# Four late heads of a clustered attention with queries on partitions, an exact maximum and weights transposed by DMA

## The chip, the cores and the metric

One core of one Trainium2 chip. The metric is the device time in microseconds. Engines are named as in the profile: PE (matmuls), DVE (vector), ACT (activations), POOL (GpSimd), SP (which issues most DMAs).

## The reference

```python
def _attn_ref(q, k, v, centroids):          # B, H, S, D = 4, 8, 768, 64; 16 centroids a head
    ...
    q_assign = np.argmax(np.einsum('bhsd,hcd->bhsc', q_n, c_n), axis=-1)
    k_assign = np.argmax(np.einsum('bhsd,hcd->bhsc', k_n, c_n), axis=-1)
    mask = q_assign[:, :, :, None] == k_assign[:, :, None, :]
    scores = scale * np.matmul(q, k.transpose(0, 1, 3, 2))
    scores = np.where(mask, scores, -1000000000.0)
    scores = scores - np.max(scores, axis=-1, keepdims=True)
    attn = np.exp(scores)
    attn = attn / (np.sum(attn, axis=-1, keepdims=True) + 1e-09)
    return np.matmul(attn, v)
def _moe_ref(x, w_in, w_spatial, b_spatial, w_out):   # x: B, 768, 512; d_ff 1024
    h = np.maximum(x @ w_in, 0.0)
    u, v = (h[..., :d_ff // 2], h[..., d_ff // 2:])
    ...                                                # v_n: v normalised over its 512 columns
    v_s = np.einsum('ts,bsd->btd', w_spatial, v_n) + b_spatial[None, :, None]
    return ((u * v_s) @ w_out)
```

The output of the attention, heads side by side, is x of the second function.

## The kernel before, in words

The work is cut into 16 pairs of heads (n = 0 to 15, four pairs a batch, head number 2n + h) and, for each batch, one gated MLP. Every f32 operand is split into two f16 halves (high and low), and a product is made of three f16 products.

For a pair, `prep` loads keys and queries (`raw`), splits them (`hq`, `lo`), computes the logits against the centroids into a PSUM bank (`misc`), takes from them one-hot rows on DVE, and writes these rows into `hq` beside the 64 columns of the head. So one matmul gives the score with a penalty where the clusters differ. For pair 0 the two heads go through this one after the other, for the others together.

`shifts` makes, for every query, a maximum that keeps the exponential in range: nine times a head PE fills a PSUM bank with f16 scores (line 817, twelve matmuls) and DVE reduces it (line 824). The result goes through ACT into small columns, is transposed by a DMA on SP, and is copied into `hq` as one more row, so that the score matmuls subtract it.

`attend` runs a head in six blocks (k) of 128 keys. PE writes scores with keys on partitions and 768 queries in columns (lines 879 and 881) into one of two two-bank PSUM tiles (`sc`), ACT takes the exponential into an f32 tile (`p32`, line 885), ACT casts it to the high half (`pt`, line 887), POOL subtracts for the low half (line 888), and PE multiplies both with the values (line 893, eighteen matmuls a block, with six more for a mean correction at k = 0), for six groups of queries in one bank. Then DVE normalises, ACT and POOL split the result (`xhl`), and SP transposes it by DMA into `xT`.

`mlp` takes `xT` of a batch: tiles of v and u (`win`), the spatial product (`wsp`), u times it on DVE, a split and a DMA transpose (`gT`; in the last batch in `pt`'s buffers), the last product (`wou`), a scaling on ACT (line 1012) and a store from ACT's queue (line 1013). MLP matmuls are issued in groups of six and stand between the attention of later batches.

What decides the order: each engine executes its instructions in the order in which they stand, and that order is the table `ORDER`, a list of operation numbers per engine, written out in the file. Buffers rotate; a DMA on SP whose data isn't ready holds everything behind it on SP.

The names that matter below: `ROW` does not exist before; `r_p32` has three tiles (`P32_BUFS`), `r_o32`, the output tile, has one; `r_gT` has three; `misc` is one bank for both heads of pair 0.

Of the kernel before, what the change touches and what calls it, by code (L numbers as in the profile page):

```python
# [1084 lines left out]
```

## Time and profile before

| | |
|---|---|
| median of 3 runs | 664.67 us (662.88 to 666.4) |
| profiled execution | 662.72 us |
| its span, first to last instruction | 660.9 us |
| mean granted clock of PE | 0.989 |
| busy: PE, DVE, ACT, POOL | 626.0, 423.0, 445.9, 425.8 us |

A busy time is the sum over the whole span; the stages of the kernel have different limits, so the table is read together with the stretches below. The 1.8 us between span and time lie around the instructions.

### The profile page before, as it was taken

What the parts mean: (1) busy time and instruction counts of PE and PEld (TensorE: products, weight loads), DVE (VectorE), ACT (ScalarE), POOL (GpSimd) and SP (SyncE); (2) the same over time, 40 slices, a digit from 0 to 9 for tenths busy, and PEclk for the clock granted to TensorE, in tenths of its full rate; (3) what the DMA queues carried; (4) which work ended last, traced back from release to release, by engine and by line L of the source; (5) the groups of instructions that cost most, each with busy time, mean ns of one, the idle gap of its engine ahead of it and who ended that gap; (6) DMA issues with size and microseconds to landing.
All of it is one profiled execution on the core that took longest, in us unless ns stands there. A gap on an engine that the chain in (4) does not pass through costs nothing.

```text
span 660.9 us, 16698 instructions
## 1 busy us (share of the span) xinstructions
PE 626.0 (95%) x6769; PEld 376.4 (57%) x6769; DVE 423.0 (64%) x835; ACT 445.9 (67%) x759; POOL 425.8 (64%) x305
## 2 busy tenths in 40 slices
PE   1897889999999999999999999999999999999997
PEld 0475557666566655567654666656645655544443
DVE  6989999999699978279775775855545511132010
ACT  3695899996789848599955997758447675323212
POOL 2265789997589937587944987758635776424111
PEclk9987999999999999999999999999999999999999
DMA  4555866578556578575754155623210322301214
GB/s 147 146 133 136 195 140 159 128 166 192 128 130 128 122 157 178 117 165 109 149 138 67 27 102 114 134 57 82 43 25 18 69 62 25 88 17 48 64 33 127
DMA packets 104349, 70.49 MB, mean 107 GB/s; under 512 B 89432, under 2 KB 90640, under 8 KB 104272
## 3 DMA queue, kind: packets, MB, share of 16 engines
q1 hardware_dynamic: 100528, 62.73, 44.1%
q10 hardware_dynamic: 3744, 6.69, 3.0%
q8 instruction: 53, 0.87, 0.5%
q14 instruction: 24, 0.20, 0.1%
HBM read 27.63 MB, written 6.29 MB: 51 GB/s over the span
## 4 chain that ended last, share of the span: by engine, by line
PE 76%; DVE 18%; ACT 2%; issue 1%; DMA 1%; POOL 0%; SPq 0%; DVEq 0%; ACTq 0%
PE acc L938 41%; PE acc L893 12%; DVE nm L824 8%; PE acc L817 7%; PE sc L879 7%; PE sc L881 7%; DVE lo L675 1%; DMA out_dram<-o 1%; ACT p L885 1%; DVE vhl L761 1%; DVE xn L914 1%; DVE acc L607 1%; PE acc L704 1%; PE acc L706 1%; DVE acc L725 1%
## 5 line engine op out<-in xcount | busy, mean ns | idle before, releaser
L888 POOL TENSOR_TENSOR pt<-p,pt 128x768 f16<-128x768 f32 x192 | 322.5, 1704 | 49.6 <-ACT pt L887 35.1
L824 DVE TENSOR_REDUCE nm<-acc 128x1 f32<-128x512 f32 (+1 forms) x288 | 183.1, 681 | 28.8 <-PE acc L817 27.4
L885 ACT ACTIVATE p<-sc 128x768 f32<-128x768 f32 x192 | 153.0, 806 | 21.8 <-PE sc L881 16.8
L887 ACT CAST pt<-p 128x768 f16<-128x768 f32 x192 | 156.3, 830 | 2.1
L893 PEld LDWEIGHTS <-pt 128*128 128x128 f16 x3456 | 128.0, 98 | 28.8 <-issue 4.5
L893 PE MATMUL acc<-vhl,pt 128*128 128x65 f16 (+1 forms) x3456 | 136.7, 194 | 0.5 <-POOL pt L888 0.4
L938 PE MATMUL acc<-win,xT 128*128 128x512 f16 x576 | 129.4, 379 | 0.0
L817 PE MATMUL acc<-hq 80*128 80x256 f16 (+1 forms) x384 | 101.2, 340 | 11.0 <-DVE nm L824 7.6
L938 PE MATMUL acc<-vn,wsp 128*128 128x512 f16 x432 | 100.1, 379 | 0.0
L879 PE MATMUL sc<-hq,lo 128*128 128x512 f16 (+1 forms) x384 | 94.8, 328 | 1.1 <-ACT p L885 1.0
L881 PE MATMUL sc<-hq 81*128 81x512 f16 (+1 forms) x384 | 95.0, 328 | 0.7 <-DVE hq L855 0.7
L938 PEld LDWEIGHTS <-xT 128*128 128x128 f16 x576 | 55.7, 98 | 65.4 <-issue 0.5
L1004 POOL TENSOR_TENSOR ghl<-u,ghl 128x512 f16<-128x512 f32 x24 | 28.9, 1203 | 69.4 <-ACT ghl L1003 53.1
L1002 DVE SCALAR_TENSOR_TENSOR u<-acc,bsp,u 128x512 f32<-128x512 f32 x24 | 18.0, 749 | 86.1 <-PE acc L938 86.0
L938 PEld LDWEIGHTS <-wsp 128*128 128x128 f16 x432 | 41.0, 97 | 46.0
L881 PEld LDWEIGHTS <-hq 81*128 81x128 f16 x384 | 37.7, 98 | 26.8 <-issue 1.7
L817 PEld LDWEIGHTS <-hq 80*128 80x128 f16 x384 | 34.2, 100 | 29.5 <-issue 13.2
L675 DVE SCALAR_TENSOR_TENSOR lo<-raw,hq 128x768 f16<-128x768 f32 x30 | 37.2, 1250 | 21.3 <-ACT hq L666 21.3
L938 PE MATMUL acc<-wou,gT 128*128 128x512 f16 x216 | 50.4, 379 | 0.0
L917 POOL TENSOR_TENSOR xhl<-xn,xhl 128x384 f16<-128x384 f32 x32 | 30.5, 954 | 26.9 <-ACT xhl L916 26.8
L879 PEld LDWEIGHTS <-lo 128*128 128x128 f16 x384 | 33.8, 98 | 23.2 <-issue 6.0
L979 POOL TENSOR_TENSOR vn<-v,vn 128x512 f16<-128x512 f32 x24 | 28.5, 1201 | 24.1 <-ACT vn L978 24.1
(112 smaller groups left out, 598.7 us busy)
## 6 DMA issues: line engine op xcount, KB each, us to landing
raw<-in_kqT_dram SPq DMA_DIRECT2D x15, 768.0 KB
vraw<-in_vp_dram SPq DMA_DIRECT2D x16, 384.0 KB
out_dram<-o ACTq DMA_DIRECT2D x24, 256.0 KB
hq<-hq SPq DMA_DIRECT2D x15, 384.0 KB
hq<-lo SPq DMA_DIRECT2D x16, 192.0 KB
lo<-hq SPq DMA_DIRECT2D x16, 192.0 KB
wraw<-in_wsT_dram SPq DMA_DIRECT2D x6, 384.0 KB
vn<-in_w_in_dram SPq DMA_DIRECT2D x4, 512.0 KB
```

Of the source, the lines that this page charges most:

```text
L675: los.append(op("DVE", 0.95, lambda h=h: V.scalar_tensor_tensor(out=lo.t[:, h, :], in0=raw.t[:, h, :], scalar=QK_SCALE, in1=hq.t[:, 0, h, ...
L817: T.matmul(out=acc.t[:, c:c + cs.stop - cs.start], lhsT=hq.t[0:R_SH, 1, h, t * P:(t + 1) * P], rhs=hq.t[0:R_SH, 0, h, cs], start=c == 0, s ...
L824: V.tensor_reduce(out=nm.t[:, t, k:k + 1] if n == 1 else nm.t[:, t:t + n, k], in_=src, axis=AX.X, op=ALU.max, negate=True)
L879: T.matmul(out=sc.t[:, cs], lhsT=lo.t[:, h, ks], rhs=hq.t[:, 2, h, cs], start=True, stop=False)
L881: T.matmul(out=sc.t[:, cs], lhsT=hq.t[0:R_E, 0, h, ks], rhs=hq.t[0:R_E, 1, h, cs], start=False, stop=True)
L885: o = op("ACT", 0.81, lambda sc=sc, p32=p32: A.activation(out=p32.t, in_=sc.t[:, 0:S], func=AF.Exp, bias=P_LOG * LN2, scale=SC_UNIT), afte ...
L887: o = op("ACT", 0.83, lambda pt=pt, p32=p32: A.copy(out=pt.t[:, 0, :], in_=p32.t), after=[o], use=[p32], new=[pt], key=K_HI)
L888: o = op("POOL", 1.65, lambda pt=pt, p32=p32: G_.tensor_tensor(out=pt.t[:, 1, :], in0=p32.t, in1=pt.t[:, 0, :], op=ALU.subtract), after=[o ...
L893: T.matmul(out=av.t[:, t * (D + 1):t * (D + 1) + w], lhsT=lhsT, rhs=rhs, skip_group_check=True, **f)
L917: xls.append(op("POOL", 0.92, lambda xn=xn, hs=hs: G_.tensor_tensor(out=xhl.t[:, :, 1, hs], in0=xn.t, in1=xhl.t[:, :, 0, hs], op=ALU.subtr ...
L938: T.matmul(out=acc.t, lhsT=lr[m][0], rhs=lr[m][1], start=(m == 0), stop=(m == n - 1))
L1004: l = op("POOL", 1.16, lambda: G_.tensor_tensor(out=ghl.t[:, 1, :], in0=u32.t, in1=ghl.t[:, 0, :], op=ALU.subtract), after=[h], use=[u32, ...
```

## The change

Four heads (25, 27, 29 and 31, the second heads of the pairs of the last batch) go another way through `attend`, and `shifts` leaves them out. PE writes their scores with 128 queries on partitions and 768 keys in columns; DVE takes the exact maximum of a block; two one-element DVE operations make from it the scale and the bias of the exponential (a scale of zero where a query has no key in its cluster); ACT and POOL make the two halves as before; SP transposes both by one DMA, 128 by 1536, back into the buffer of the f32 tile; PE takes the transposed halves as its stationary operand, eighteen matmuls a block. The mean correction is not made for these heads. There is a fourth `p32` tile. The logits of pair 0's second head go into a bank of their own. A half copy of `hq` in pair 0 now reads ACT's copy. The output tile is gone: the scaled output is written over the `gT` tile that PE has read. The order of all engines is new.

```diff
-P32_BUFS = 3
+P32_BUFS = 4
...
-O_BUFS = 1
+ROW = (25, 27, 29, 31)
...
 ORDER = {
...
+    r_rs = R(sm, "rs", [P, 4], F32, 4)
...
-    r_o32 = R(moe, "o32", [P, DM], F32, O_BUFS)
...
-            qa2 = [sp(lambda: nc.sync.dma_start(out=hq.t[0:D, 2], in_=hq.t[D:P, 0]), 0.9, after=his, use=[hq], key=KQ)]
+            qa2 = [sp(lambda: nc.sync.dma_start(out=hq.t[0:D, 2], in_=hq.t[0:D, 1]), 0.9, after=qa0, use=[hq], key=KQ)]
...
+            if one and not first:
+                misc = r_acc.new()
...
         for h in range(2):
+            if 2 * n + h in ROW:
+                continue
             nm, sx = r_nm.new(), r_shx.new()
...
-            for k in range(NT):
+            for k in range(NT if 2 * n + h in ROW else 0):
+                plan.due = due(n, (6 * h + k) / 12)
+                sc, p32, pt, rs = r_sc.new(), r_p32.new(), r_pt.new(), r_rs.new()
+
+                def scores(sc=sc, h=h, k=k):
+                    ks = slice(k * P, (k + 1) * P)
+                    for cs in halves:
+                        T.matmul(out=sc.t[:, cs], lhsT=hq.t[:, 2, h, ks], rhs=lo.t[:, h, cs], start=True, stop=False)
+                    for cs in halves:
+                        T.matmul(out=sc.t[:, cs], lhsT=hq.t[0:R_SH, 1, h, ks], rhs=hq.t[0:R_SH, 0, h, cs], start=False, stop=True)
+
...
+                o = op("DVE", 0.95, lambda sc=sc, rs=rs: V.tensor_reduce(out=rs.t[:, 0:1], in_=sc.t[:, 0:S], axis=AX.X, op=ALU.max, negate=True), after=[o], use=[sc], new=[rs], key=K_MAX)
+                o = op("DVE", 0.16, lambda rs=rs: V.tensor_scalar(out=rs.t[:, 1:2], in0=rs.t[:, 0:1], scalar1=LIM, scalar2=SC_UNIT, op0=ALU.is_lt, op1=ALU.mult), after=[o], use=[rs], key=K_MAX)
+                o = op("DVE", 0.16, lambda rs=rs: V.tensor_scalar(out=rs.t[:, 2:3], in0=rs.t[:, 0:1], scalar1=rs.t[:, 1:2], scalar2=P_LOG * LN2, op0=ALU.mult, op1=ALU.add), after=[o], use=[rs], key=K_MAX)
+                o = op("ACT", 0.81, lambda sc=sc, p32=p32, rs=rs: A.activation(out=p32.t, in_=sc.t[:, 0:S], func=AF.Exp, bias=rs.t[:, 2:3], scale=rs.t[:, 1:2]), after=[o], use=[sc, rs], new=[p32], key=K_EXP)
...
+                o = op("POOL", 1.65, lambda pt=pt, p32=p32: G_.tensor_tensor(out=pt.t[:, 1, :], in0=p32.t, in1=pt.t[:, 0, :], op=ALU.subtract), after=[o], use=[p32, pt], key=K_LO)
+
+                def rt(p32=p32):
+                    return p32.t.bitcast(F16).rearrange("p (j q) -> p j q", q=P)
+
+                o = sp(lambda pt=pt, rt=rt: nc.sync.dma_start_transpose(rt(), pt.t.rearrange("p a s -> p (a s)")), 1.95, after=[o], use=[pt, p32], turn=True, key=K_XD)
+
+                def values(av=av, rt=rt, h=h, k=k):
...
+                    for j in range(NT):
+                        mm(j, D + 1, vh.t[:, j, h, 0:D + 1], start=k + j == 0, stop=False)
+                        mm(j, D, vh.t[:, j, h, D + 2:], start=False, stop=False)
+                        mm(NT + j, D + 1, vh.t[:, j, h, 0:D + 1], start=False, stop=j == NT - 1)
...
+            for k in range(0 if 2 * n + h in ROW else NT):
...
-            o32 = r_o32.new()
+
+            def o32():
+                return gT.t.rearrange("p a s -> p (a s)")[:, 0:2 * DM].bitcast(F32)
+
...
-            o = op("ACT", 0.6, lambda: A.activation(out=o32.t, in_=acc.t, func=AF.Copy, scale=2.0 ** -(G_LOG + WOUT_LOG)), after=[o], use=[acc], new=[o32], key=T_O)
-            op("ACT", 0.06, lambda: A.dma_start(out=out[b, t * P:(t + 1) * P, :], in_=o32.t), after=[o], use=[o32], dma=0.8, key=0)
+            o = op("ACT", 0.6, lambda: A.activation(out=o32(), in_=acc.t, func=AF.Copy, scale=2.0 ** -(G_LOG + WOUT_LOG)), after=[o], use=[acc, gT], key=T_O)
+            op("ACT", 0.06, lambda: A.dma_start(out=out[b, t * P:(t + 1) * P, :], in_=o32()), after=[o], use=[gT], dma=0.8, key=0)
```

The rest of the diff is the new table and some cost numbers of the planner that prints it; the table alone decides the order. Three places show how the order moves. Lines of the changed kernel are some 2 to 40 higher than those of the same code before (675 stays, 723 to 727 become 725 to 729, 824 becomes 828, 858 and 859 become 862 and 863, 919 becomes 958, 1005 becomes 1044).

The first is DVE at the start of the program, from the chain on the centroids' norms (p_114 holds the centroids) to the first one-hot steps on the logits. Before:

```order
L559 TENSOR_SCALAR p_114<-p_114,ninv 128x128
L675 SCALAR_TENSOR_TENSOR lo<-raw,hq 128x768
L568 CAST cmh<-acc_110 64x2x16
...
L569 TENSOR_TENSOR cml<-acc_110,cmh 64x6x16
L675 SCALAR_TENSOR_TENSOR lo<-raw,hq 128x768
L723 TENSOR_REDUCE mx<-acc_111 128x12
L724 TENSOR_TENSOR acc_111<-acc_111,mx 128x12x16
L725 TENSOR_TENSOR acc_111<-acc_111,wt 128x12x16
L723 TENSOR_REDUCE mx<-acc_111 128x12
```

And of the change:

```order
L559 TENSOR_SCALAR p_114<-p_114,ninv 128x128
L675 SCALAR_TENSOR_TENSOR lo<-raw,hq 128x768 x2
L568 CAST cmh<-acc_110 64x2x16
...
L569 TENSOR_TENSOR cml<-acc_110,cmh 64x6x16
L725 TENSOR_REDUCE mx<-acc_111 128x12
L726 TENSOR_TENSOR acc_111<-acc_111,mx 128x12x16
L727 TENSOR_TENSOR acc_111<-acc_111,wt 128x12x16
L725 TENSOR_REDUCE mx<-acc_112 128x12
```

The second low half stands directly behind the first, ahead of the placing of the centroids (cmh, cml), and the second head's logits are read from a second bank (acc_112).

The second place is DVE in the last batch, at the second head of pair 14 (head 29). Before, these are the last of its reductions and the step that joins them:

```order
L824 TENSOR_REDUCE nm_90<-acc_112 128x2
L824 TENSOR_REDUCE nm_90<-acc_111 128x1
L785 TENSOR_SCALAR wh_92<-acc_113 2x2x64
L824 TENSOR_REDUCE nm_90<-acc_110 128x1
L786 SCALAR_TENSOR_TENSOR w_8741<-acc_113,wh_92 2x2x64
L824 TENSOR_REDUCE nm_90<-acc_110 128x2
L836 TENSOR_REDUCE nl<-nm_90 128x6
```

In the change, behind the step that joins the first head's of pair 15:

```order
L840 TENSOR_REDUCE nl<-nm_90 128x6
L887 TENSOR_REDUCE rs<-sc_108 128x1
L888 TENSOR_SCALAR rs<-rs 128x1
L889 TENSOR_SCALAR rs<-rs 128x1
L887 TENSOR_REDUCE rs<-sc_109 128x1
L787 TENSOR_SCALAR wh_92<-acc_110 2x2x64
L951 TENSOR_SCALAR rc<-acc_111 128x6
L888 TENSOR_SCALAR rs<-rs 128x1
L952 RECIPROCAL rc<-rc 128x6
L889 TENSOR_SCALAR rs<-rs 128x1
```

The reductions from the four banks (acc) are gone; DVE now stands between the scores (sc) and the exponential, with three instructions a block.

The third place is SP at the end of the last batch, pair 15. Before:

```order
L788 DMA mean_86<-wh_92 1x2x65
L858 DMA_TRANSPOSE sht<-shx_84 128x6x128
L1005 DMA_TRANSPOSE gT<-ghl 128x8x128
L859 DMA hq<-sht 3x768
L789 DMA mean_86<-wl_94 1x2x65
L919 DMA_TRANSPOSE xT_104<-xhl 128x12x128
L1005 DMA_TRANSPOSE gT<-ghl 128x8x128 x3
L919 DMA_TRANSPOSE xT_104<-xhl 128x12x128
```

And of the change (p_9059 and the like are the f32 tiles that take the transposed halves):

```order
L1044 DMA_TRANSPOSE gT<-ghl 128x8x128
L958 DMA_TRANSPOSE xT_104<-xhl 128x12x128
L898 DMA_TRANSPOSE p_9059<-pt 128x12x128
L898 DMA_TRANSPOSE p_9092<-pt 128x12x128
L898 DMA_TRANSPOSE p_9143<-pt 128x12x128
L1044 DMA_TRANSPOSE gT<-ghl 128x8x128
L898 DMA_TRANSPOSE p_9163<-pt 128x12x128
L898 DMA_TRANSPOSE p_9206<-pt 128x12x128
L898 DMA_TRANSPOSE p_9279<-pt 128x12x128
L1044 DMA_TRANSPOSE gT<-ghl 128x8x128
L958 DMA_TRANSPOSE xT_104<-xhl 128x12x128
```

Six transposes of the late head stand between the xT transposes of pairs 14 and 15, with two of the MLP's among and behind them; the shift's transpose and row copy of that head are gone.

## Rows read from the trace of the kernel before

**Rows 1.** Stretches: window, length, each engine's busy us (instructions), PEclk, DMA share, GB/s.

```profile
20.00:153.00 133.00, 118.91 (x1674) 81.71 (x1673) 127.77 (x233) 114.86 (x203) 104.39 (x66) 0.95 0.63 148
153.00:437.00 284.00, 282.25 (x3330) 174.96 (x3329) 215.08 (x400) 219.29 (x371) 212.01 (x142) 1.00 0.60 127
437.00:570.00 133.00, 133.00 (x1314) 76.87 (x1311) 50.77 (x106) 81.49 (x134) 85.03 (x62) 1.00 0.21 45
570.00:656.70 86.70, 86.66 (x402) 39.11 (x400) 16.93 (x41) 21.03 (x37) 19.93 (x19) 1.00 0.26 63
```

**Rows 2.** Timeline of PE, 455 to 458 us: start us, us, engine, line, operation.

```profile
455.88 0.59 PE L817 MATMUL acc<-hq 80*128 80x512 f16 x2
456.31 0.34 PE L893 MATMUL acc<-mean,hq 83*128 83x65 f16 x6
456.49 0.71 PE L893 MATMUL acc<-vhl,pt 128*128 128x65 f16 x18
457.04 0.49 PE L879 MATMUL sc<-hq,lo 128*128 128x512 f16 x2
...
457.70 0.38 PE L817 MATMUL acc<-hq 80*128 80x256 f16 x2
457.92 0.26 PE L893 MATMUL acc<-vhl,pt 128*128 128x65 f16 x3
```

**Rows 3.** Groups by line: operands, count, busy us, mean ns, idle before and its releaser.

```profile
L888 POOL TENSOR_TENSOR pt<-p,pt 128x768 f16<-128x768 f32 x192 | 322.5, 1704 | 49.6 <-ACT pt L887 35.1 <-issue 3.6 <-PE sc L881 2.8
...
L887 ACT CAST pt<-p 128x768 f16<-128x768 f32 x192 | 156.3, 830 | 2.1
L885 ACT ACTIVATE p<-sc 128x768 f32<-128x768 f32 x192 | 153.0, 806 | 21.8 <-PE sc L881 16.8 <-POOL pt L888 3.9 <-ACT o L1012 0.4
...
L621 DVE TENSOR_SCALAR bsp<-bsp 128x6 f32<-128x6 f32 x1 | 1.6, 1611 | 0.0
...
L855 DVE TENSOR_TENSOR hq<-sc,hq 19x768 f16<-19x768 f32 x1 | 1.0, 955 | 0.0
```

**Rows 4.** Timeline of the start, DVE and POOL.

```profile
5.83 0.98 POOL L544 MEMSET ohx<- 128x768 f16 x2
...
6.47 0.15 DVE L557 TENSOR_SCALAR nrm<-nrm 128x1 f32<-128x1 f32 x1
...
7.06 0.95 DVE L675 SCALAR_TENSOR_TENSOR lo<-raw,hq 128x768 f16<-128x768 f32 x1
...
9.82 1.59 POOL L759 TENSOR_TENSOR vhl<-vraw,vhl 128x768 f16<-128x768 f32 x1 [2.38 <-ACT vraw L758]
10.10 2.12 DVE L675 SCALAR_TENSOR_TENSOR lo<-raw,hq 128x768 f16<-128x768 f32 x1
...
13.35 0.37 DVE L724 TENSOR_TENSOR acc<-acc,mx 128x192 f32<-128x192 f32 x1 [0.74 <-PE acc L706]
...
19.55 0.67 DVE L824 TENSOR_REDUCE nm<-acc 128x1 f32<-128x512 f32 x1
```

**Rows 5.** Timeline around the xT transposes of pairs 10 and 15 (SPq: SP's queue).

```profile
399.83 1.44 SPq L919 DMA_TRANSPOSE xT<-xhl  x1
...
406.24 0.51 ACT L916 CAST xhl<-xn 128x384 f16<-128x384 f32 x1 [1.21 <-DMA xT<-xhl]
...
568.11 1.79 PE L893 MATMUL acc<-vhl,pt 128*128 128x65 f16 x54
...
573.77 1.44 SPq L919 DMA_TRANSPOSE xT<-xhl  x1
```

**Rows 6.** Stretches behind the last xT transpose, columns as in rows 1.

```profile
573.80:576.80 3.00, 3.00 (x15) 1.37 (x14) 0.39 (x1) 0.00 (x0) 0.00 (x0) 1.00 0.84 187
576.80:577.80 1.00, 1.00 (x7) 0.47 (x5) 0.36 (x1) 0.00 (x0) 0.00 (x0) 1.00 0.05 8
```

**Rows 7.** Timeline of the end.

```profile
646.14 10.52 PE L938 MATMUL acc<-wou,pt 128*128 128x512 f16 x48
...
657.22 0.60 ACT L1012 ACTIVATE o<-acc 128x512 f32<-128x512 f32 x1 [2.16 <-DMA out_dram<-o]
```

More of the change, by code (lines that the diff above doesn't have):

```diff
@@ L530, in cr @@
         return scratch.t[:, 3 * D + P:4 * D + P]
-    ld_c = op("SP", 0.6, lambda: nc.sync.dma_start(out=cr(), in_=cent), new=[scratch], dma=1.5, key=KC)
+    ld_c = op("SP", 0.6, lambda: nc.sync.dma_start(out=cr(), in_=cent), new=[scratch], dma=1.95, key=KC)
     ld_i = op("SP", 0.6, lambda: nc.sync.dma_start(out=idt(), in_=ident), use=[scratch], dma=0.1, key=KC)
@@ L620, in late_weights @@
         ld = op("ACT", 0.06, lambda: A.dma_start(out=bsp, in_=b_sp), dma=0.1, at=40.0)
-        o = op("DVE", 0.18, lambda: V.tensor_scalar(out=bsp, in0=bsp, scalar1=2.0 ** (WS_LOG + VN_LOG), scalar2=None, op0=ALU.mult), after=[ld])
+        o = op("DVE", 0.18, lambda: V.tensor_scalar(out=bsp, in0=bsp, scalar1=2.0 ** (WS_LOG + VN_LOG), scalar2=None, op0=ALU.mult), after=[ld], port=True)
         w_ops["bsp"] = [o]
@@ L659, in prep @@
         if n == 0:
-            raws = [move(("ACT", "SP")[h], lambda q, h=h: q.dma_start(out=raw.t[:, h, :], in_=kqT[b, p, :, h, :]), use=[raw] if h else [], new=[] if h else [raw], dma=1.8, key=KP) for h in range(2)]
+            raws = [move(("ACT", "SP")[h], lambda q, h=h: q.dma_start(out=raw.t[:, h, :], in_=kqT[b, p, :, h, :]), use=[raw] if h else [], new=[] if h else [raw], dma=(0.02, 1.6)[h], key=KP) for h in range(2)]
         else:
             raws = [sp(lambda: nc.sync.dma_start(out=raw.t, in_=kqT[b, p]), 3.7, new=[raw], at=A_R4 if n == 4 else 0.0, key=KP)] * 2
-        ldv = sp(lambda: nc.sync.dma_start(out=vraw.t, in_=vp[b, p]), 2.2, new=[vraw], key=KV)
+        ldv = sp(lambda: nc.sync.dma_start(out=vraw.t, in_=vp[b, p]), 2.2 if n else 0.9, new=[vraw], key=KV)
         his, los = [], []
@@ L696, in prep, with logits @@
             half = 0.365 if one else 0.555
-            def logits(part=part):
+            if one and not first:
+                misc = r_acc.new()
+            def logits(part=part, misc=misc):
                 lgv = misc.t[:, cs].rearrange("p (t a h c) -> p t a h c", a=2, h=2, c=C)
@@ L706, in logits, with lgf @@
                         T.matmul(out=o, lhsT=hq.t[:, 0, h, ts], rhs=cml[:, 2 * p + h], start=False, stop=True)
-            lg = op("PE", 0.46 * len(part), logits, after=his[hs] + los[hs] + c_cm[0:1 if n == 0 else 2], use=[hq, lo] + ([] if first else [misc]), new=[misc] if first else [], cols=576 * len(part), key=T_LG + lt)
+            lg = op("PE", 0.46 * len(part), logits, after=his[hs] + los[hs] + c_cm[0:1 if n == 0 else 2], use=[hq, lo], new=[misc], cols=576 * len(part), key=T_LG + lt)
             lgs.append(lg)
-            def lgf(hs=hs):
+            def lgf(hs=hs, misc=misc):
                 return misc.t[:, cs].rearrange("p (n h c) -> p n h c", h=2, c=C)[:, :, hs]
@@ L747, in prep @@
                 continue
-            tr = last["oht"] = sp(lambda: nc.sync.dma_start_transpose(oht.t, ohx.rearrange("p t x c -> p (t x c)")), 0.95, after=[k1, k2], new=[oht], turn=True, key=KP + T_OT)
+            tr = last["oht"] = sp(lambda: nc.sync.dma_start_transpose(oht.t, ohx.rearrange("p t x c -> p (t x c)")), 1.1, after=[k1, k2], new=[oht], turn=True, key=KP + T_OT)
             for x in range(4):
                 m = C if x > 1 else C + 1
-                rows.append(sp(lambda x=x, m=m: nc.sync.dma_start(out=hq.t[R_OH:R_OH + m, x // 2, x % 2, :], in_=oht.t[2 * x * C:2 * x * C + m].rearrange("c t s -> c (t s)")), 0.6, after=[tr, lg] + qa0, use=[hq, oht], key=KR))
+                rows.append(sp(lambda x=x, m=m: nc.sync.dma_start(out=hq.t[R_OH:R_OH + m, x // 2, x % 2, :], in_=oht.t[2 * x * C:2 * x * C + m].rearrange("c t s -> c (t s)")), 0.75, after=[tr, lg] + qa0, use=[hq, oht], key=KR))
         lo1 = sp(lambda: nc.sync.dma_start(out=lo.t[D:P], in_=hq.t[0:D, 0]), 0.9, after=[qa1] + lgs, use=[lo, hq], key=KQ)
```

8 lines of the change are left out of this document (7 added, 1 removed), and 132 rows, old and new, of the table ORDER.

## The prediction

> **What bounds the kernel now.** An average over a kernel of several stages proves little, so I read the table of stretches first, then single timelines. From 20 to 153 us DVE is busy 127.77 of 133 us and PE only 118.91: here DVE sets the pace (the per-query maxima). From 153 to 437 us PE is busy 282.25 of 284 us, from 437 to 570 us 133.00 of 133, from 570 to 656.7 us 86.66 of 86.70, always at a granted clock of 1.00, the upper of its two levels [rows 1]. So from 153 us on every matmul that leaves PE's queue shortens the kernel by its own length, as long as nothing new makes PE wait. The late heads that the change touches lie between 437 and 570 us, where DVE is busy only 50.77 us and the DMA share is 0.21: there is room for more DVE and DMA work. What is left is the first 20 us, a chain of short steps, and the last 4.2 us behind PE's last matmul.
>
> **The change, part by part.** The sum is made against the profiled execution: 660.9 us of span, 662.72 us with the 1.8 us around it. It lies at the low end of the three runs shown (662.88 to 666.4, median 664.67).
>
> *Late heads, what goes.* For four heads the pass of maxima disappears: twelve matmuls a head on PE, six of 512 and six of 256 columns. In the PE-bound stage two of 512 take 456.31 - 455.88 = 0.43 us from start to start, two of 256 take 457.92 - 457.70 = 0.22 us [rows 2]. (A row's own duration contains the pipelining and would overstate it.) So 3 x 0.43 + 3 x 0.22 = 1.95 us a head, 7.8 us for four. The six matmuls of the mean correction take 456.49 - 456.31 = 0.18 us a head [rows 2], 0.7 us for four. Scores (four matmuls, 457.70 - 457.04 = 0.66 us) and values (eighteen, 457.04 - 456.49 = 0.55 us) keep number and width. **PE loses 8.5 us**, all of it on the path. DVE loses nine reductions a head, ACT three short columns, SP a transpose and a row copy; none was on the path there, I cost them at nothing.
>
> *Late heads, what comes.* Per block of 128 queries DVE takes a maximum over 768 columns in PSUM. The trace has none of that width; another 768-wide DVE read of PSUM took 0.955 us [rows 3], a 512-wide reduction 0.67 [rows 4]: I take 0.95. Two one-element operations for the scale and the bias of the exponential follow; between the nearest rows, 0.15 us [rows 4] and, at six elements, 1.61 us [rows 3], I take 0.15 for each (reasons below). DVE's load a head is 6 x (0.95 + 0.3) = 7.5 us against 9 x 0.67 = 6.0; its idle time hides that. The exponential with scale and bias per partition isn't in the trace; its plain form takes 0.81 us, the cast 0.83, POOL's subtraction 1.70 [rows 3]. I take 0.81 (not less; not more than a second pass of 0.83).
>
> The new thing is the transpose by DMA, 24 of them, 128 by 1536, the size of the one that feeds xT. The last of those was issued at 573.77 us [rows 5], and the DMA share, 0.84 over the next 3.0 us, falls to 0.05 from 576.80 us [rows 6]: 3.1 us to landing, at most 0.84 x 3.0 = 2.5 us of all engines. In a stretch with other loads a waiter was released 406.24 - 399.83 = 6.4 us after issue [rows 5]. I take 3.1, since the late stretch has a third of the DMA share of the stage before it [rows 1].
>
> From the end of a block's scores to its values: 0.95 + 0.3 + 0.81 + 0.83 + 1.70 + 3.1 = 7.7 us, with handoffs some 8.1; before it was 0.81 + 0.83 + 1.70 = 3.3. PE doesn't stand still if its queue holds other work in between. In the new PE order I counted it with 0.66 us for scores, 0.55 for values [rows 2] and, for six MLP matmuls, an eighth of 10.52 us for 48, 1.3 [rows 7]: between scores and values stand 9.4 us for the very last block, 10.2 to 15.4 for 22 others, 23 for one. The latency is covered with 1.3 us to spare at the tightest. I put **1.5 us** for stalls where POOL or SP has another instruction first; bounds 0 (the cover holds) and 12 (rival one). With no cover each head would pay about 8.1 - 3.3 = 4.8 us.
>
> The f32 weight tile is now held until the values, 0.81 + 0.83 + 1.70 + 3.1 + 0.55 = 7.0 us, with four tiles 1.75 us a block. PE's work around a late head's six blocks is over 25 us by the same count. That hides it.
>
> After the last values PE needs work until xT of the last pair has landed; before, the values ended at 568.11 + 1.79 = 569.90 us [rows 5] and xT landed at 576.8, 6.9 us later. Seven groups of six MLP matmuls stood there (9.1 us), now six (7.8): covered, by 0.9 us.
>
> *The start.* DVE's second low half (L675) started at 10.10 us beside POOL's 1.59 us at 9.82 and took 2.12 us; the first took 0.95 [rows 4]. It now stands directly behind the first, at about 8.0 us, done before POOL starts: 1.2 us won. With each head's logits in a bank of its own, DVE's second step, which sat idle 0.74 us behind PE's logits [rows 4], has no such wait: 0.7 us. The identity cast leaves the front: I count nothing (0 to 0.6). The centroids are placed 0.95 us later than before, which DVE, in order, has already paid for in the first item. So the first maximum, at 19.55 us [rows 4], comes some 1.9 us earlier. DVE carries the stage to 153 us with 5.2 us idle, so most of this should arrive where PE takes over: **1.5 us** (0 to 2.6). The half copy of hq that now waits for ACT's copies is needed at the first scores, later than 30 us; it costs nothing.
>
> *The end.* The output tile had one buffer: ACT sat 2.16 us behind the last but one store and began the last scaling at 657.22 us, 0.56 us after PE's last matmul (646.14 + 10.52 = 656.66) [rows 7]. Now each tile lies in a buffer that PE has done with: **0.5 us** (0.4 to 0.6). That buffer is held a store longer, 2.2 us, behind six groups of PE work (7.8 us); nothing.
>
> *The order* of the middle is new throughout. PE has 284 - 282.25 = 1.75 us of idle time there to win [rows 1] and no bound on what it may lose; I take nothing.
>
> Sum: 662.7 - 7.8 - 0.7 - 1.5 - 0.5 + 1.5 = 653.7, **654 us**.
>
> **A rule against the change.** While POOL was in its subtractions a DVE scaling of 128 by 6 elements took 1.61 us [rows 3]; one of 128 by 1 took 0.15 us at 6.47 us, inside a POOL fill of 0.98 us that began at 5.83 [rows 4]. The new operations have one element too, so I take 0.15. The Trainium skill, "SBUF — State Buffer", section "SBUF: two separate sides", says that DVE and GpSimd share a pair of ports as an exclusive lock, so that a DVE operation in a two-port mode waits for the whole GpSimd instruction. The 1.61 us row agrees; the 0.15 us row speaks for one element not taking the lock, though no run here shows it beside a subtraction. By the rule the time would be rival one's; by the one-element row it is the sum above.
>
> **The rivals.** *One: the scale waits for POOL.* Both small operations wait for a whole subtraction of 1.70 us, 3.4 us more a block, 11.5 us instead of 8.1. The blocks of a head shift together, so PE pays once a head, the largest shortfall against the cover counted above: 0, 1.0, 1.3 and 2.1 us for the four heads, 4 us together; with 2 us more of queueing behind other POOL work, 12. Time 656 to 664, middle 660. For it: the 1.61 us row. Against it: the 0.15 us row.
>
> *Two, slower than before: the transposes become the bound.* From the first scores to the last values of a late head PE has 25 to 36 us of work; 5 us of it pass before the first transpose. In the other 20 us SP's queue must move six of these and one gT, so the bound is passed at 20 / 7 = 2.9 us apiece. If issue and move overlap, the row says at most 2.5 us; if the next issue (1.44 us [rows 5]) waits for the move, 1.44 + 2.5 = 3.9 us: each head then loses 7 x 1.0 = 7 us, 28 in all, 682 us. The gain is gone from 3.2 us apiece on. Against it: the 2.5 us is an upper bound, since the 0.84 holds whatever else moved in those 3 us.
>
> *Three: the start and the new order give nothing.* PE's 8.5 us are won, but the DVE stage swallows the start, and the reordered middle idles PE 6 to 8 us more: 661 to 664.
>
> **How the numbers follow.** Forecast 0.68, rival one 0.10, two 0.07, three 0.15. With all gains at their upper bounds and no stall, 662.7 - 8.5 - 2.6 - 0.6 - 1.75 = 649.2: low end 649. The high end, 663, takes in rival one and most of three and leaves out two. A measurement of this kernel tells 0.5%, 3.3 us, from no change. Faster than 661.3 us: 0.68, most of rival one, a third of three: 0.80. Within: 0.13. Slower: 0.07, rival two.
>
> **What would show it.** Right: 336 matmuls of the maxima instead of 384, PE idle under 4 us between 153 us and its last matmul, the first maximum near 17.7 us, the last scaling within 0.1 us of PE's end. Wrong: PE waiting in the late heads for the transposed weights by more than 6 us in all; the one-element operations at 1 us and more; transposes spaced by more than 2.9 us; or PE idle in the middle, where it was full.

## The result, and the profile after

The changed kernel takes 654.82 us (median of 4, 654.11 to 655.43) against 663.77 us before (4 runs, 661.97 to 666.4): ratio 0.9878, 95% interval 0.9843 to 0.9913. The prediction said 654 (649 to 663). Repeated beside before on two more chips, it took 656.98 us (ratio 0.9936, 0.9907 to 0.9965) and 655.92 us (ratio 0.9918, 0.9887 to 0.995). The numbers differ between chips as executions differ in PE's mean granted clock: on those two chips, executions of before at 1.00 took 659.2 to 659.6 us and of the changed kernel 653.7 to 655.8, while lower clocks, down to 0.98, came with up to 666.4 and 661.4 (not in step: before also took 659.65 us at 0.986). At the upper level throughout (2.4 GHz), the gain is thus 3.4 to 5.9 us. The first comparison shows 8.95; there the changed kernel ran at 1.00 and the profiled execution of before at 0.989.

The profiled execution took 654.74 us, its span is 653.0 us. Its stretches, columns as in [rows 1], with the sum up to 153 us ahead:

```profile
0.00:153.00 153.00, 128.37 (x1821) 86.89 (x1822) 141.07 (x297) 126.43 (x221) 110.55 (x86) 1.00 0.62 155
153.00:437.00 284.00, 281.00 (x3226) 171.56 (x3223) 209.20 (x395) 217.43 (x368) 209.94 (x143) 1.00 0.57 127
437.00:562.00 125.00, 123.02 (x1228) 70.91 (x1227) 57.14 (x135) 83.83 (x122) 82.33 (x60) 1.00 0.57 107
562.00:649.30 87.30, 86.77 (x433) 39.58 (x430) 16.53 (x41) 21.22 (x38) 19.91 (x19) 1.00 0.30 65
```

The same first stretch of the kernel before, and within it the 6 us ahead of a fall of the granted clock and 6 us behind it:

```profile
0.00:153.00 153.00, 124.13 (x1732) 85.49 (x1733) 140.17 (x289) 123.45 (x217) 108.85 (x84) 0.96 0.62 149
26.00:32.00 6.00, 4.71 (x56) 3.12 (x55) 5.84 (x12) 1.65 (x5) 1.60 (x1) 1.00 0.91 229
33.00:39.00 6.00, 5.89 (x27) 3.53 (x27) 5.04 (x10) 5.44 (x11) 3.24 (x2) 0.50 0.48 100
```

Two things are to be read. From 153 us to the end of PE's last matmul PE now sits idle 3.0 + 1.98 + 0.53 = 5.5 us; before it was 1.8 [rows 1]. (In the two other profiled executions of the changed kernel, `after_again` and `after_third`, it was 5.1 and 4.8.) And PE has done 4.2 us more by 153 us, at a clock of 1.00, where before was granted 0.50 (1.2 GHz) from 33 to 39 us, after a stretch in which PE had been busy 4.71 of 6 us, and again from 57 to 63.

Groups by line, which answer to [rows 3]:

```profile
L821 PE MATMUL acc<-hq 80*128 80x256 f16 (+1 forms) x336 | 89.8, 338 | 11.6 <-DVE nm L828 8.9 <-DVE xn L953 0.4 <-ACT ohx L737 0.4
...
L890 ACT ACTIVATE p<-sc,rs 128x768 f32<-128x768 f32 x24 | 23.6, 989 | 13.2 <-DVE rs L889 9.2 <-POOL pt L893 2.7 <-DVE rs L888 0.9
L887 DVE TENSOR_REDUCE rs<-sc 128x1 f32<-128x768 f32 x24 | 22.9, 953 | 21.5 <-PE sc L884 21.4
...
L889 DVE TENSOR_SCALAR rs<-rs 128x1 f32<-128x1 f32 x24 | 4.9, 210 | 0.6
...
L888 DVE TENSOR_SCALAR rs<-rs 128x1 f32<-128x1 f32 x24 | 3.4, 146 | 0.4
```

There are 336 matmuls of the maxima, as predicted. The maximum over 768 took 0.953 us (taken: 0.95) and the two one-element operations 0.15 and 0.21 (taken: 0.15 each); the exponential with scale and bias per partition took 0.99, not 0.81.

The start, beside [rows 4], and the end, beside [rows 7]:

```profile
5.87 0.29 DVE L559 TENSOR_SCALAR p<-p,ninv 128x128 f32<-128x128 f32 x1
6.08 1.91 DVE L675 SCALAR_TENSOR_TENSOR lo<-raw,hq 128x768 f16<-128x768 f32 x2
...
10.29 0.37 DVE L726 TENSOR_TENSOR acc<-acc,mx 128x192 f32<-128x192 f32 x1
...
16.10 0.69 DVE L828 TENSOR_REDUCE nm<-acc 128x1 f32<-128x512 f32 x1 [0.27 <-PE acc L821]
...
638.69 10.52 PE L977 MATMUL acc<-wou,pt 128*128 128x512 f16 x48
...
649.25 0.60 ACT L1054 ACTIVATE pt<-acc 128x512 f32<-128x512 f32 x1 [1.19 <-PE acc L977]
```

Both low halves now run in 1.91 us together, the second step has no wait, and the first maximum stands at 16.10 us, 3.45 earlier. Part of the 3.45 is the execution: with the old start the first maximum stood at 18.42 (`end_alone`), 18.89 (`late_and_end`) and 19.55 us (before), with the new one between 16.10 and 16.64 in eleven profiled executions. The last scaling starts 0.04 us behind PE's last matmul (638.69 + 10.52 = 649.21).

Where PE waits for the new weights, in the chain that ended last (start, length, what) and in PE's waits from 437 to 650 us (us in total, times, longest):

```profile
518.67 5.44 DMA p<-pt
524.15 0.72 PE acc L902 x18
...
568.37 6.16 DMA xT<-xhl
574.58 5.57 PE acc L977 x25
```

```profile
PE acc L902 <- DMA p<-pt: 1.5, 1, 1.5
PE acc L977 <- DMA xT<-xhl: 0.4, 1, 0.4
PE sc L882 <- ACT p L890: 0.4, 1, 0.4
```

One transposed block of head 29 landed 5.4 us after its issue and the last xT 6.2 us after, where 3.1 was taken for both [rows 5, 6]; PE stood still 1.5 and 0.4 us. The first is no accident of this execution: the same block landed 5.3 and 5.4 us after its issue in `after_again` and `after_third`, and PE waited 1.4 and 1.5 us for it. The wait for xT was not there in either.

### The profile page after: what moved, and what is told of

Same layout as the page of the kernel before. It is cut to its first block, busy times and chain, and to the rows that moved or that the text cites. A ratio compares the mean times of both kernels' runs of the same rounds, so it can differ in the third digit from the quotient of the medians.

```text
span 653.0 us, 16609 instructions
## 1 busy us (share of the span) xinstructions
PE 619.2 (95%) x6697; PEld 368.9 (57%) x6697; DVE 423.9 (65%) x867; ACT 449.5 (69%) x747; POOL 422.7 (65%) x305
## 4 chain that ended last, share of the span: by engine, by line
PE 69%; DVE 15%; ACT 6%; DMA 3%; issue 3%; POOL 2%; SPq 0%; ACTq 0%; POOLq 0%; DVEq 0%
PE acc L977 39%; PE acc L932 9%; DVE nm L828 8%; PE sc L918 5%; PE sc L920 5%; PE acc L821 4%; ACT pt L926 2%; ACT p L924 2%; PE acc L902 2%; DVE lo L675 1%; POOL pt L927 1%; PE sc L882 1%; PE sc L884 1%; DMA xT<-xhl 1%; DMA p<-pt 1%
## 5 line engine op out<-in xcount | busy, mean ns | idle before, releaser
L828 DVE TENSOR_REDUCE nm<-acc 128x1 f32<-128x512 f32 (+1 forms) x252 | 160.7, 683 | 30.7 <-PE acc L821 29.3
L924 ACT ACTIVATE p<-sc 128x768 f32<-128x768 f32 x168 | 133.9, 808 | 24.9 <-PE sc L920 20.6
L926 ACT CAST pt<-p 128x768 f16<-128x768 f32 x168 | 137.0, 832 | 2.5 <-ACT gT L1054 0.7
L932 PEld LDWEIGHTS <-pt 128*128 128x128 f16 x3024 | 109.3, 97 | 21.6 <-issue 4.2
L932 PE MATMUL acc<-vhl,pt 128*128 128x65 f16 x3024 | 117.2, 193 | 1.7 <-POOL pt L927 1.5
L821 PE MATMUL acc<-hq 80*128 80x256 f16 (+1 forms) x336 | 89.8, 338 | 11.6 <-DVE nm L828 8.9
L920 PE MATMUL sc<-hq 81*128 81x512 f16 x336 | 83.6, 330 | 1.0 <-DMA hq<-sht 0.8
L918 PE MATMUL sc<-hq,lo 128*128 128x512 f16 x336 | 83.4, 330 | 0.9 <-ACT p L924 0.4
L920 PEld LDWEIGHTS <-hq 81*128 81x128 f16 x336 | 33.1, 98 | 24.4 <-issue 2.6
L918 PEld LDWEIGHTS <-lo 128*128 128x128 f16 x336 | 29.4, 98 | 24.4 <-issue 8.9
```

The source lines that it names most:

```text
L821: T.matmul(out=acc.t[:, c:c + cs.stop - cs.start], lhsT=hq.t[0:R_SH, 1, h, t * P:(t + 1) * P], rhs=hq.t[0:R_SH, 0, h, cs], start=c == 0, s ...
L828: V.tensor_reduce(out=nm.t[:, t, k:k + 1] if n == 1 else nm.t[:, t:t + n, k], in_=src, axis=AX.X, op=ALU.max, negate=True)
L918: T.matmul(out=sc.t[:, cs], lhsT=lo.t[:, h, ks], rhs=hq.t[:, 2, h, cs], start=True, stop=False)
L920: T.matmul(out=sc.t[:, cs], lhsT=hq.t[0:R_E, 0, h, ks], rhs=hq.t[0:R_E, 1, h, cs], start=False, stop=True)
L924: o = op("ACT", 0.81, lambda sc=sc, p32=p32: A.activation(out=p32.t, in_=sc.t[:, 0:S], func=AF.Exp, bias=P_LOG * LN2, scale=SC_UNIT), afte ...
L926: o = op("ACT", 0.83, lambda pt=pt, p32=p32: A.copy(out=pt.t[:, 0, :], in_=p32.t), after=[o], use=[p32], new=[pt], key=K_HI)
```

## The experiments

Twelve kernels ran, four on each of three chips; those on one chip share the runs of before. Theories: the gain is PE's removed matmuls and what was predicted around them, or it comes from elsewhere (start, order, clock) while the late heads pay for their new waits.

### The end alone

```diff
-            o32 = r_o32.new()
+            def o32():
+                return gT.t.rearrange("p a s -> p (a s)")[:, 0:2 * DM].bitcast(F32)
```

> The kernel before with one edit: the scaled output rows lie in the gT tile that PE has done with, in place of the single output buffer. By the sum of the prediction it is 0.4 to 0.6 us faster than before (662.7 to 662.2), and ACT's last scaling starts within 0.1 us of PE's last matmul in place of 0.56 us behind it. The rival is that the longer hold of gT makes PE wait for a gT tile somewhere earlier, so that the time doesn't change or grows; then PE shows waits for gT that it had not before.

659.91 us against 661.36: ratio 0.998 (0.9964 to 0.9997), so 0.2 to 2.4 us. The timeline of its end:

```profile
654.78 2.75 PE L937 MATMUL acc<-wou,pt 128*128 128x512 f16 x12
...
657.57 0.60 ACT L1014 ACTIVATE pt<-acc 128x512 f32<-128x512 f32 x1 [1.99 <-PE acc L937]
```

PE ends at 657.53 and the span at 661.3, 3.8 us later (4.2 before): 0.4 us, as predicted, without new waits of PE behind 153 us.

### The start alone

```diff
+            if one and not first:
+                misc = r_acc.new()
-            def logits(part=part):
+            def logits(part=part, misc=misc):
...
-... in_=hq.t[D:P, 0]), 0.9, after=his, use=[hq], key=KQ)]
+... in_=hq.t[0:D, 1]), 0.9, after=qa0, use=[hq], key=KQ)]
```

> The kernel before with the new start alone: the first logits in two banks, the half copy of hq behind ACT's copies, and the new order of each engine for what starts in the first 30 us; the rest stands in the order of before. The first maximum was at 19.55 us before and 16.10 after. Theory one, the stage up to 153 us is a DVE queue with almost no slack, so a start that is 3.45 us earlier arrives nearly whole: 2.5 to 3.5 us faster. Theory two, the prediction's own size: 1.5 us. Theory three, the stage swallows it because other waits (transposed rows, loads) come last further on: within 0.5 us of before.

660.37 us against 661.36: ratio 0.9988 (0.9961 to 1.0014). That excludes a whole 3 us in the median, and leaves 1.5 and 0 open. The profiled execution, at 0.994, has a span of 657.7 us, the first maximum at 16.52 us and PE's last matmul ending at 653.26, where before it ended at 656.66 and in `end_alone`, with the same old start, at 657.53; PE is idle 1.75 or 1.76 us behind 153 us in all three; its busy time up to 153 us, the first number behind the comma, is 128.44, against 124.13 before:

```profile
0.00:153.00 153.00, 128.44 (x1776) 87.28 (x1776) 141.84 (x293) 125.62 (x221) 112.60 (x85) 0.98 0.63 154
```

So the stage doesn't swallow the start in this execution. But five of the twelve executions had a mean clock under 0.99 and took 661.9 to 665.7 us, so a lowered clock can hide what the start wins. Among those at 0.993 and more, a choice made afterwards, seven with the new start have a median of 659.5 us and fifteen of before 661.1: 1.6 us.

### Late heads and end, without the new start and middle

The changed kernel with the edits of the start undone and the order of before for what starts before 400 us.

> The changed kernel with the old start and the old order for all that starts before 400 us: the four late heads, the fourth weight tile and the new end alone. Theory one, PE is the bound there and loses 8.5 us of matmuls, the end gives 0.5, the new waits cost up to 2: 7 to 9 us faster than before. Theory two, a good part of the 9 us that were measured comes from the order of the middle and the start: less than 6 us faster.

657.23 us against 661.36: ratio 0.9943 (0.9922 to 0.9964), 3.8 us, not 7 to 9. Its stretches from 153 us on:

```profile
153.00:437.00 284.00, 279.54 (x3267) 172.28 (x3266) 209.35 (x392) 217.25 (x366) 207.97 (x142) 1.00 0.60 126
437.00:562.00 125.00, 122.75 (x1227) 70.74 (x1226) 59.17 (x143) 84.45 (x124) 84.73 (x61) 1.00 0.58 109
562.00:653.10 91.10, 91.03 (x468) 41.85 (x466) 17.28 (x42) 23.45 (x41) 21.82 (x20) 1.00 0.30 69
```

PE's idle time there is 4.5 + 2.25 + 0.07 = 6.8 us, 5.0 more than before. -8.5 - 0.5 + 5.0 = -4.0: the matmuls are won, and half is given back in waits (2.2 us of them between 380 and 400 us, where the two orders meet).

### The maxima's matmuls put back, idle

```diff
+                    for cs in halves:
+                        T.matmul(out=sc.t[:, cs], lhsT=hq.t[0:R_SH, 1, h, ks], rhs=hq.t[0:R_SH, 0, h, cs], start=True, stop=True)
                     for cs in halves:
                         T.matmul(out=sc.t[:, cs], lhsT=hq.t[:, 2, h, ks], ..., start=True, stop=False)
```

> The changed kernel with twelve idle matmuls a late head put back, six of 512 and six of 256 columns, as wide as those of the maxima that the change removed (two ahead of each block's scores, their result is overwritten). Theory one, PE is the bound in the late stretch and its work passes one to one into the time: 7.8 us slower than the changed kernel (7.3 to 8.3), near 662.6. Theory two, the late heads are bound by the way from a block's scores over the maximum and the transpose to its values, so PE has room: 0 to 4 us slower, and PE's waits for the transposed weights shrink or vanish.

660.38 us against 661.36: ratio 0.9994 (0.9979 to 1.0009). Beside the changed kernel's ratios of 0.9918 and 0.9936 on two other chips that is 3.8 to 5.0 us slower, between the two theories; the profiled spans, both at a clock of 1.00, are 658.0 and 653.0 us, 5.0 apart. The stretch of the late heads:

```profile
437.00:562.00 125.00, 124.67 (x1246) 72.46 (x1244) 57.36 (x137) 82.12 (x119) 81.87 (x59) 1.00 0.58 103
```

PE's idle time in it falls from 1.98 to 0.33 us and its wait for the transposed weights from 1.5 to 0.3: part of the 7.8 us filled gaps that PE had anyway.

### The order of the middle undone

The changed kernel with the order of before for what starts between 30 and 400 us.

> The changed kernel with the order of before for all that starts between 30 and 400 us: new start, late heads, fourth tile and new end, without the new order of the middle. Theory one, the order between 30 and 153 us keeps PE so fed that the clock isn't lowered, and it is this that was won beyond the prediction's start: 1.5 to 4 us slower than the changed kernel, with stretches of granted clock 0.5 between 30 and 80 us. Theory two, what was predicted: the order of the middle is worth nothing, within 1 us of the changed kernel. Theory three, the new order costs PE idle time between 153 and 437 us (3.0 us shown in place of 1.75), so the old one is 1 to 2 us faster.

655.07 us, ratio 0.9916 (0.9887 to 0.9946), beside 656.98 and 0.9936 (0.9907 to 0.9965) for the changed kernel on the same chip:

> The changed kernel once more, unaltered, beside before and three variants, so that all are compared on one chip. By the accounts so far (654.8 us against 663.8 on one chip, where before lost clock between 20 and 80 us, and 661.4 for before on another) it is 6 to 9 us faster than before, at a granted clock of 1.00 in nearly every run, while before shows 0.97 to 1.00.

The two can't be told apart. The first theory falls: the old order isn't slower, and it is the changed kernel that was at 0.99 and under in six of twelve executions here, 658.4 to 660.4 us, and at 653.7 to 655.5 in the others; two of the twelve with the old order were. That also misses what was expected of the changed kernel on this chip, a clock of 1.00 in nearly every run and 6 to 9 us over before, where the medians give 4.3.

### Six elements in place of one

```diff
-... out=rs.t[:, 1:2], in0=rs.t[:, 0:1], scalar1=LIM, ...
-... out=rs.t[:, 2:3], in0=rs.t[:, 0:1], scalar1=rs.t[:, 1:2], ...
+... out=rs.t[:, 6:12], in0=rs.t[:, 0:6], scalar1=LIM, ...
+... out=rs.t[:, 12:18], in0=rs.t[:, 0:6], scalar1=rs.t[:, 6:7], ...
```

> The changed kernel with the two small operations of DVE on 128 by 6 elements in place of 128 by 1 (the maximum is taken over six parts of the keys; the scale and bias come from the first part alone, so this kernel leaves out the maximum over the other five). Theory one, width decides: operations of this width wait for POOL's subtraction as the one of 128 by 6 at 1.61 us did before, so most of these 48 take 0.5 to 1.8 us, PE waits for late weights, and the kernel is 2 to 8 us slower than the changed one. Theory two, such small operations don't wait for POOL whatever their width: 0.15 to 0.25 us each and no change of the time.

DVE's maximum gives six numbers here, one for each of six parts of the keys; scale and bias come from the first alone, the other five are left out. 659.91 us, ratio 0.9991 (0.9962 to 1.0021): 2.9 us slower than the changed kernel by the medians on this chip. Those medians mix clocks; at 0.999 and more, five executions here took 658.95 to 659.97 us and three of the changed kernel 653.74 to 654.58, 4.4 to 6.2 us apart. The two operations in its groups by line, then two places of its timeline where they meet a subtraction:

```profile
L889 DVE TENSOR_SCALAR rs<-rs 128x6 f32<-128x6 f32 x24 | 14.9, 624 | 0.6
...
L888 DVE TENSOR_SCALAR rs<-rs 128x6 f32<-128x6 f32 x24 | 11.7, 490 | 0.4
```

```profile
434.10 1.64 POOL L893 TENSOR_TENSOR pt<-p,pt 128x768 f16<-128x768 f32 x1
434.20 1.56 DVE L889 TENSOR_SCALAR rs<-rs 128x6 f32<-128x6 f32 x1
...
438.57 1.64 POOL L893 TENSOR_TENSOR pt<-p,pt 128x768 f16<-128x768 f32 x1
438.71 1.53 DVE L888 TENSOR_SCALAR rs<-rs 128x6 f32<-128x6 f32 x1
```

And the timeline of the changed kernel, where the one-element operation starts inside a subtraction:

```profile
435.93 1.65 POOL L893 TENSOR_TENSOR pt<-p,pt 128x768 f16<-128x768 f32 x1
436.07 0.14 DVE L888 TENSOR_SCALAR rs<-rs 128x1 f32<-128x1 f32 x1
```

Width decides. In these rows the operation on six elements ends with POOL's instruction, and the one on one element passes beside it. This is what the prediction took from a single row beside a fill [rows 4].

### Each transpose twice

```diff
+                    nc.sync.dma_start_transpose(rt(), pt.t.rearrange("p a s -> p (a s)"))
                     return nc.sync.dma_start_transpose(rt(), pt.t.rearrange("p a s -> p (a s)"))
```

> The changed kernel with each of the 24 transposes by DMA issued twice, the second time with the same source and goal, so that the DMA engines move 24 more blocks. By the prediction's second rival the bound is passed when a block's transposes take more than 2.9 us of SP's queue and of the engines; two of them take 2 x 1.44 us to issue and an estimated 2 x 1.9 to 2.5 us of all engines (from the DMA share). Theory one, the transposes have no slack beyond that: 3.8 to 5 us a block, each late head loses 6 to 14 us, and the kernel is 20 to 50 us slower. Theory two, the cover by MLP matmuls holds most of it: 0 to 10 us slower.

726.63 us, ratio 1.0989 (1.0938 to 1.1039): 70 us slower than the changed kernel, 2.9 us for each added transpose. PE's stretch from 437 us to the end, here and in `after_again`, and 10 us within it:

```profile
437.00:722.50 285.50, 230.46 (x1677) 117.39 (x1677) 73.69 (x176) 105.94 (x159) 101.74 (x78) 0.92 0.52 102
437.00:652.80 215.80, 210.18 (x1676) 111.01 (x1672) 73.92 (x179) 106.11 (x160) 102.78 (x78) 1.00 0.45 91
500.00:510.00 10.00, 5.60 (x31) 2.58 (x30) 1.09 (x3) 2.68 (x4) 5.46 (x4) 0.50 0.65 117
```

So not all of the 70 us is transposing: PE stands idle 55.0 us in place of 5.6, and the same matmuls keep it busy 230.5 us in place of 210.2, at a mean clock of 0.92 in place of 1.00. Some 49 us are waits, 2.1 for each added transpose, and 20 are longer busy time, which goes with the clock; it stood at 0.50 in stretches where PE waited, as from 500 to 510 us. PE's waits, then three blocks in the timeline:

```profile
PE acc L906 <- DMA p<-pt: 51.8, 20, 5.7
```

```profile
486.58 1.16 PE L906 MATMUL acc<-vhl,p 128*128 128x65 f16 x18 [2.97 <-DMA p<-pt]
487.83 0.99 ACT L890 ACTIVATE p<-sc,rs 128x768 f32<-128x768 f32 x1 [3.28 <-PE acc L906]
...
492.35 0.72 PE L906 MATMUL acc<-vhl,p 128*128 128x65 f16 x18 [1.63 <-DMA p<-pt]
...
499.25 0.71 PE L906 MATMUL acc<-vhl,p 128*128 128x65 f16 x18 [2.29 <-DMA p<-pt]
```

A block now takes 5.8 to 6.9 us. The loss is over both expected ranges, the waits alone at the upper end of the first: the transpose holds the values, the values hold the f32 tile, and ACT's next exponential waits for that tile. The rate by which the prediction weighed this rival, 2.9 us apiece, bounds it only from below. In the changed kernel the DMA share between 437 and 562 us rose from 0.21 [rows 1] to 0.57, (0.57 - 0.21) x 125 = 45 us for the 21 transposes issued in it: an estimate of 2.1 us apiece, under 2.9 with little to spare. The added transposes give the same: (0.52 x 285.5 - 0.45 x 215.8) / 24 = 2.1 us.

### Three forms of the exponential

```diff
+                    if k % 3 == 0:
+                        A.activation(..., func=AF.Exp, bias=rs.t[:, 2:3], scale=rs.t[:, 1:2])
+                    elif k % 3 == 1:
+                        A.activation(..., func=AF.Exp, bias=rs.t[:, 2:3], scale=SC_UNIT)
+                    else:
+                        A.activation(..., func=AF.Exp, bias=P_LOG * LN2, scale=SC_UNIT)
```

> The changed kernel with the exponential of the late heads in three forms: blocks 0 and 3 of a head with scale and bias per partition as in the change, blocks 1 and 4 with the bias per partition and a constant scale, blocks 2 and 5 with both constant (these two thirds leave out the scale, or the scale and the maximum). Theory one, the operand per partition is what makes 0.99 us of the 0.81 predicted: 0.99, then 0.81 to 0.99, then 0.81 in the third form. Theory two, it is the late stretch (DVE reading the same banks, DMA writing weights) that slows it: 0.99 in all three. The time stays within 1 us of the changed kernel in both, since ACT has slack there.

655.37 us, ratio 0.9906 (0.9882 to 0.9929), as the changed kernel on the same chip (655.92). Its groups by line, in the order of the diff:

```profile
L892 ACT ACTIVATE p<-sc,rs 128x768 f32<-128x768 f32 x8 | 7.9, 989 | 3.1 <-DVE rs L889 1.5 <-DVE rs L888 0.9 <-POOL xhl L964 0.8
L894 ACT ACTIVATE p<-sc,rs 128x768 f32<-128x768 f32 x8 | 7.2, 898 | 4.5 <-DVE rs L889 3.9 <-POOL pt L901 0.5
L896 ACT ACTIVATE p<-sc 128x768 f32<-128x768 f32 x8 | 6.4, 805 | 4.4 <-DVE rs L887 2.7 <-issue 1.7
```

Each operand per partition costs 0.09 us; the late stretch costs nothing. The Trainium skill, "ScalarE: Activation LUTs", section "What ACT_TABLE_LOAD costs", gives about 93 ns for each pointer operand; the rows agree.

### The wait at 524 us, and a better order

One group of six MLP matmuls (operation 679 in PE's order) is moved ahead of the values of head 29's third block (808).

```diff
-678 813 808 815 679 696
+678 813 679 808 815 696
```

> The changed kernel unaltered, as the measure for the next two: 653.7 to 655.5 us in executions at a granted clock near 1.00, 658 to 660 at 0.99, 4 to 9 us faster than before on the same chip.

> The changed kernel with one group of six MLP matmuls placed ahead of the values of the third block of head 29, where PE sat 1.5 us for the transposed weights at 524 us in the changed kernel. Theory one, that wait is latency that the order of PE left uncovered: it goes, and the kernel is 1.2 to 1.7 us faster. Theory two, the transposes are bound by the rate of the DMA engines there: the wait moves to the next block's values and nothing is won.

654.33 us, ratio 0.9902 (0.9878 to 0.9925), against 655.92 and 0.9918 for the changed kernel. PE's wait for the weights shrinks from 1.5 to 0.3 us without coming back at the next block, the row of PE's waits behind 153 us now being

```profile
PE acc L902 <- DMA p<-pt: 0.3, 1, 0.3
```

The intervals overlap, so the 1.2 us are shown by the wait, and the time (1.6 us by the medians) doesn't show them.

> The same move, and the order of before for what starts between 30 and 300 us. Theory one, the order of before idles PE a little less there (1.75 us against 2.26 shown between 153 and 300) and the moved group saves 1.5: 2 us faster than the changed kernel, near 652 at full clock. Theory two, the middle order is worth nothing and only the moved group counts: 1.5 us. In both the executions with a lowered clock between 30 and 80 us come oftener than in the changed kernel.

Here the order of before also stands for what starts between 30 and 300 us. 651.86 us, ratio 0.9866 (0.984 to 0.9892): 1.3% faster than before, 4.1 us faster than the changed kernel by the medians on this chip (the intervals just touch), and the best of all. Its stretches from 153 us:

```profile
153.00:437.00 284.00, 281.72 (x3241) 172.48 (x3240) 207.24 (x394) 218.97 (x368) 208.12 (x143) 1.00 0.58 128
437.00:562.00 125.00, 124.56 (x1251) 71.86 (x1250) 57.66 (x138) 82.01 (x120) 82.22 (x59) 1.00 0.58 107
```

PE's idle time in the two is 2.28 + 0.44 = 2.7 us, in the changed kernel 5.0. Its six executions stood at 0.993 to 0.997, the changed kernel's eight at 0.989 to 1.00. In the two profiled executions PE's last matmul ends 4.0 us earlier (644.05 and 648.09 us): 2.1 of it is less idle time behind 153 us, 0.5 less before it, and 1.5 less busy time for the same matmuls. What makes the last two, no run isolates.

## Why the prediction was right

The total was right, but not by the sum alone: two of its terms were off in opposite directions, and its starting point was lucky. The sum is reckoned from an execution of before at 662.72 us and a clock of 0.989; on the next two chips before had medians of 661.3 and 661.5 us, and the gain was 4.3 and 5.6 us, where the sum has 8.7. The changed kernel's own time, 654.8 to 657.0 us, lies in the range on all three chips. In the two profiled executions, whose spans differ by 660.9 - 653.0 = 7.9 us:

| term | predicted | measured | read from |
|---|---|---|---|
| PE's matmuls in the late heads | -8.5 | -6.9 in this pair | PE busy 626.0 to 619.2 |
| waits of PE from 153 us on | +1.5 | +3.7 | idle 1.8 to 5.5 |
| up to 153 us | -1.5 | -4.2 | PE busy 124.1 to 128.4 |
| end | -0.5 | -0.4 | 4.2 to 3.8 behind PE's last matmul |

The measured terms make -6.9 + 3.7 - 4.2 - 0.4 = -7.8. One pair of executions is a coarse measure of such terms, since PE's busy time in three executions of the changed kernel alone was 616.9, 619.0 and 619.2 us.

**PE's matmuls.** Right: count and widths are as taken. The three profiled kernels with the old late heads (before, `end_alone`, `start_alone`) have PE busy 626.0, 628.4 and 626.9 us, a mean of 627.1; the nine with the new ones and nothing doubled or put back have 615.5 to 620.5, a mean of 618.8. That is 8.3 us less, against the 8.5 of the sum.

**"I put 1.5 us for stalls"** is the first term mis-sized. The block of the late heads was costed nearly as it runs (0.95 + 0.15 + 0.21 + 0.99 + 0.83 + 1.64 us, the exponential 0.18 above the 0.81 taken), but the landing of 3.1 us was one row taken as if it held for all 24, and the row of 6.4 us [rows 5] was set aside. It was 5.4 us for the third block of head 29, in each of three executions of the changed kernel, and that block cost 1.5 us. The chain behind the last values, given a margin of 0.9 us, ended 574.57 - (565.00 + 0.71) = 8.9 us after them in place of 6.9, and PE waited 0.4. The rest lies elsewhere: PE's idle time between 153 and 437 us, where the sum took nothing, rose from 1.75 to 3.0 us, which is the written sign "PE idle in the middle" in a weak form. The sign that was written down, PE idle under 4 us, failed at 5.5. `group_earlier` shows that the large wait was uncovered latency, since most of it went with one group of cover; `maxima_back` shows the same from the other side.

**"1.5 us (0 to 2.6)" for the start** is the second. Against the profiled execution of before the two causes acted as costed (1.91 us for both low halves, no wait at the second step). But the first was a matter of which engine came first. In `end_alone`, with the old start, DVE began its second low half (there line 674) just ahead of POOL, took 0.96 us and not 2.12, and POOL was the one that took longer:

```profile
10.13 0.96 DVE L674 SCALAR_TENSOR_TENSOR lo<-raw,hq 128x768 f16<-128x768 f32 x1
10.22 2.31 POOL L758 TENSOR_TENSOR vhl<-vraw,vhl 128x768 f16<-128x768 f32 x1 [2.74 <-ACT vraw L757]
```

There the first maximum stood at 18.42 us, 1.13 earlier than in before, without any new start. The cause counted at nothing, the identity cast out of the way of the centroids, was worth 1.0 us in this pair: line 559 starts at 5.87 instead of 6.86, and at 5.8 to 6.4 in the other executions with the new start. So the first maximum came 1.8 to 3.45 us earlier, by the executions compared, with 1.9 put for it. The 4.2 us up to 153 us contain more than the start: before was profiled with two stretches of about 6 us at 0.50. `start_alone`, profiled with one such stretch, ends PE's work 3.4 us earlier than before, but its median is only 1.0 us better; what part is clock stays open.

**The end** and **the order of the middle** (0) came out as put: `end_alone` and `old_middle`. That another order is worth more, `best_order` suggests; the prediction gave PE's 1.75 us there as all that could be won, which is idle time behind 153 us only.

**Rival one** (the scale waits for POOL) was real and didn't happen: `six_wide` makes it happen and takes 659.9 us, where the prediction had put 656 to 664, middle 660. The rule cited against the change, the Trainium skill, "SBUF — State Buffer", section "SBUF: two separate sides", agrees with the rows at six elements; at one element the operation didn't wait. The Trainium skill, "VectorE: DVE Perf Modes", section "What auto-detection actually checks", ties the two-port mode for one source in SBUF to outermost dimensions that are even or equal; the rows at six agree, of a single element that section says nothing, and other widths weren't tried.

**Rival two** (the transposes become the bound) was nearer than its 0.07: 2.1 us apiece against a bound of 2.9. Past it `double_turn` loses more than the rate alone gives: 6 x 4.2 + 2.1 - 20 = 7.3 us a head, 29 in all with the gT at 2.1 too, against 49 us of waits.

**Rival three** had PE idle 6 to 8 us more in the middle and the start lost. The first half came about in part (3.7); the start, not swallowed in the profiled executions, paid for it.

Open: why those two transposes landed late. The one of head 29 did so, at 5.2 to 5.6 us, in `old_middle`, `exp_forms`, `group_earlier` and `late_and_end` as well, so it goes with its place in the order. In both, a stretch of some 1 us shows a DMA share above 1, so that transfers overlap in the count:

```profile
570.00:571.20 1.20, 1.20 (x8) 0.52 (x6) 0.66 (x2) 0.62 (x1) 0.03 (x1) 1.00 1.88 51
521.50:522.50 1.00, 1.00 (x7) 0.39 (x4) 0.00 (x0) 0.69 (x1) 0.97 (x1) 1.00 2.78 188
522.50:523.50 1.00, 0.12 (x2) 0.00 (x0) 0.78 (x1) 0.00 (x0) 1.00 (x2) 1.00 0.05 5
```

It looks as if a few long packets held some engines (share 2.78, then 0.05 at 5 GB/s) while the transpose waited for its last part. That is argued and not shown, and which packets they were, no run settles.
